# Four low parts of weights on GpSimd, and chunk sums and gated-unit matmuls in fixed turns on TensorE

## The chip, the core and the metric

The kernel runs on one core of one Trainium2 chip. The metric is the device time of one execution in microseconds (us), the median of several. Engines are named as in the profile: PE is TensorE (PEld its weight loads), DVE is VectorE, ACT is ScalarE, POOL is GpSimd, SP is SyncE. Matmuls read their operands from SBUF and write PSUM. Each engine carries out its own queue of instructions in the order in which it was built; an instruction that waits for another engine holds up everything behind it in its queue.

## What is computed

A layer norm of `u` (2048 x 448) feeds two branches whose results are added to `u`:

```python
x  = A_u                       # (1, 2048, 448)
xn = layernorm(x)
# branch A: diagonal state-space convolution, N = 256 states a channel
A  = -exp(log_A_real) + 1j*A_imag;  C = (C_real + 1j*C_imag)*dt
K  = 2*einsum("dn,dnl->dl", C, exp(A*dt*pos)).real      # 448 kernels of length 2048
yA = irfft(rfft(xn, 4096)*rfft(K, 4096))[:2048] + xn*D_skip
# branch B: gated unit, F = 1792
yB = (sigmoid(xn @ w_gate) * (xn @ w_up)) @ w_down
out = x + yA + yB
```

## The kernel before

All matmuls run on values split into a high part, rounded to the `fp32r` format, and a low part, the difference, and add three products (high by high, high by low, low by high).

Two Python generators, `conv()` and `glu()`, put out the work of the branches. The loop at the end of the kernel takes a step of the one that lags behind its share; the number that each `yield` gives says how much work the step held (`WK` = 5.5 for a chunk of `kgen`). A scheduler then makes the order of each engine's queue. It follows the program's order where priorities are equal, but lets an instruction overtake another that it thinks is not ready yet; `hp()` lifts priorities, and `tc.issue_after(ins)` says that an instruction must be queued on its engine behind `ins`. It adds no wait of its own; waits come from the data.

**Branch B** (`glu`, `gate`). The 1792 hidden units come in 14 tiles `f` of 128, in five groups of 3, 3, 3, 3 and 2. The tokens come in two halves of two blocks `t`. In the first half the weights of each tile are loaded into `wraw` (one buffer), ACT makes the high part `wh`, and DVE makes the low part `wl` (L752; L750 for the first tile). In the second half the tiles of `RAW` are loaded again and POOL makes both (L758, L759); the others come back from HBM. `gate` computes one tile for one block: 11 matmuls `gu` for the gate and 11 for the other factor (L698), each group of 11 into one of four PSUM banks shared under the tag `gu`; ACT makes `th`, DVE `hf` (L709), ACT `hh` and DVE `hl` (L716). After a group's tiles, `po` (L811) multiplies by `w_down`, and DVE adds the bank to `acc` (L816).

**Branch A** starts with `prep`, in which DVE and ACT make the parameters of the 448 kernels, and `x_spec`. Then `kgen` makes the kernels in 56 chunks of 8 channels. For chunk `cn`:

- `ahead(cn + 1)`: PE forms phases in `tr` (L526, four matmuls of 512 columns, one PSUM buffer), and ACT takes sines of them into `S` (L535 to L538, two buffers);
- POOL makes magnitudes `me` and `mf` for two chunks at a time (L491, L503), with squares on ACT (L516); once in 8 chunks (`c == 4`) DVE makes `powers` for the next 8 (L440, ten instructions) that those start from;
- DVE multiplies magnitudes and sines: `Et` (L589, L590; two buffers) and `Ft` (L591; one buffer), called the products here;
- PE sums them over the states: `ko`, 32 small matmuls in four column groups (L603), called the chunk's sums;
- after each fourth chunk the bank `ko` is copied, and later `first_stage` puts out 32 matmuls `kp`, `kq` (L553).

A `yield WK / 2` stands between `ahead` and the products, and another after the sums:

```python
                yield WK / 2
                Et = tl[f"Et{cn % 2}"]
                Ft = tl["Ft"]
...
                yield WK / 2
```

Last comes `spectra` (L893, L920, L955), in which the frequency products are formed and transformed back. There the two branches' matmuls already take turns: `sp_mm` holds the last matmul of the branch A, `glu_mm` that of the branch B, each side is queued behind the other with `issue_after`, and the list `glu_on`, filled at the first step of `spectra`, switches this on in `gate` and in the `po` loop.

Of the kernel before, what the change touches and what calls it, by code (L numbers as in the profile page):

```python
# [15 lines left out]
ALU = mybir.AluOpType  # L16
# [13 lines left out]
WK = 5.5  # L30
# [2 lines left out]
WS = 4.5  # L33
WP = 5
WX = 2
HELD = 12.6
HP = 300
Y0 = (8, 1)
# [9 lines left out]
DC = 8  # L48
# [82 lines left out]
def s4d_glu_kernel(ctx, tc, io):  # L131
    nc = tc.nc
    hp = tc.high_priority
    v = nc.vector
# [148 lines left out]
    def x_spec(xn, b0):  # L283

        for p in range(2):
# [7 lines left out]
            for i in range(2):  # L293
                r = row(b0 + i, 2 * p)
                nc.scalar.dma_start(x1_d[:, r : r + 9 : 8], x1[64 * i : 64 * i + 64])
            yield WX

# [147 lines left out]
    def kgen(pk):  # L445
# [72 lines left out]
        def ahead(cn):  # L518
# [19 lines left out]
            sins[:] = [nc.scalar.activation(cs, cs, AF.Sin, scale=-TWO_PI, bias=hpi)]  # L538
            return S

        def first_stage(bank):

            ks, sk = tl["ks"], tl["sk"].rearrange("p k (s r j) -> p r k s j", r=2, j=2)

            pss = [
                psc[-1].tile([128, 8, 2, 32], F32, name="kp", bufs=1),
                psg.tile([128, 8, 2, 32], F32, name="kq", tag="gu", bufs=4),
            ]
            for s_ in range(8):
                for cc in range(2):  # L550
                    for r in range(2):
                        rows = slice(64 * r, 64 * r + 64)
                        nc.tensor.matmul(  # L553
                            pss[r][64 * cc : 64 * cc + 64, s_].rearrange("p j k -> p (j k)"),
                            ks[rows, s_], wk[rows, cc], start=True, stop=True,
                            skip_group_check=True,
                        )
            for r in range(2):
                nc.scalar.copy(sk[:, r], pss[r].rearrange("p s j k -> p k s j"))
            sk_to = sk_d[:, bank // 7, :, bank % 7]  # L560
            nc.scalar.dma_start(sk_to, tl["sk"].rearrange("p (g k) e -> p g (k e)", k=4))
# [11 lines left out]
        for g in range(NCK // NCH):  # L573
            for c in range(NCH):
                cn = g * NCH + c
                S = nxt
                me, mf = (m[:, 2 * DC * (c % 2) : 2 * DC * (c % 2) + 2 * DC] for m in mags)
                if c == 4 and NCH * (g + 1) < NCK:
                    with tc.issue_after(fts[0].ins):
                        powers(pms, g + 1, sins[0])  # L580
                if cn + 1 < NCK:
                    nxt = ahead(cn + 1)
                    if c % 2 == 1:
                        squares(coming[0])
                yield WK / 2
                Et = tl[f"Et{cn % 2}"]
                Ft = tl["Ft"]
                two = lambda ap: ap.unsqueeze(1).to_broadcast([128, 2, 2 * DC, 32])
                v.tensor_tensor(Et[:, :, :, 32:64], two(me[:, :, 32:64]), S[:, 1::-1], ALU.mult)  # L589
                v.tensor_tensor(Et[:, :, :, 0:32], two(me[:, :, 0:32]), S[:, 1:3, :, ::-1], ALU.mult)  # L590
                fts[:] = [v.tensor_tensor(Ft, two(mf), S[:, 3:5], ALU.mult)]  # L591
                if cn + 2 < NCK and c % 2 == 0:
                    coming = magnitudes(cn // 2 + 1)
                if c % 2 == 1:
                    mags = coming
                if cn % 4 == 0:
                    ko = psc[-1].tile([128, 8, 64], F32, name="ko", bufs=1)
                for q in range(2):
                    sl = 2 * (cn % 4) + q
                    for k in range(4):  # L600
                        h, cc = k // 2, k % 2
                        for j in range(4):
                            mm = nc.tensor.matmul(  # L603
                                ko[32 * j : 32 * j + 32, sl],
                                Ft[:, cc, DC * h + 4 * q + j],
                                Et[:, cc, DC * h + 4 * q + j],
                                start=(k == 0),
                                stop=(k == 3),
                                skip_group_check=True,
                            )  # L610
                if cn % 4 == 3:
                    ks = tl["ks"]
                    nc.tensor.matmul(
                        ko[:, :, 0], ident, dm[:, cn // 4], start=False, stop=True, skip_group_check=True
                    )
                    nc.scalar.copy(ks, ko)
                yield WK / 2
                if cn % 4 == 2 and cn > 3 or cn + 1 == NCK:

                    with hp(HP) if cn + 1 == NCK else tc.issue_after(glu_mm[0].ins):  # L620
                        first_stage((cn - 3) // 4 if cn + 1 < NCK else cn // 4)
# [18 lines left out]
    def w_low():  # L640
        return pg.tile([128, 2, 4, 128], F32R, name="wl", bufs=2)
# [77 lines left out]
    def glu():  # L719
        for half in range(2):  # L720
# [4 lines left out]
            for fs_ in ORDER[half]:  # L725
# [14 lines left out]
                for n_, (f, t) in enumerate(order):  # L740
                    if t == 0:
                        wh = pg.tile([128, 2, 4, 128], F32R, name="wh", bufs=2)
                        if half == 0:
                            first = len(raws) == 2
                            raw, rd = raws.pop() if raws else (w_load(f), None)
                            wl = w_low()
                            with hp(HP):
                                nc.scalar.copy(wh, raw)
                                if first:
                                    v.scalar_tensor_tensor(wl, raw, lim[:, 0, 0:1], wh, ALU.mult, ALU.subtract)  # L750
                                else:
                                    v.tensor_tensor(wl, raw, wh, ALU.subtract)  # L752
                            if f not in RAW:
                                for t_, d_ in kept((wh, wl), wt_d, f):
                                    nc.sync.dma_start(d_, t_)
                        elif f in RAW:
                            raw, wl = w_load(f, eng=nc.gpsimd), w_low()
                            nc.gpsimd.tensor_copy(wh, raw)  # L758
                            nc.gpsimd.tensor_tensor(wl, raw, wh, ALU.subtract)  # L759
                        else:  # L760
                            wl = w_low()
                            for t_, d_ in kept((wh, wl), wt_d, f):
                                nc.sync.dma_start(t_, d_)
                        ws.append((wh, wl))
                    between = (lambda s_=mid[n_]: step(*s_)) if cross and mid[n_] else None

                    yield from gate(ws[f - f0], xq[2 * half + t], hs[t], between, half == 0 and (f, t) == (1, 0))
                    if t == 0:
                        dh = pg.tile([128, D], F32R, name="dh", bufs=FCH[0])
                        if half == 0:  # L770
                            rd = rd or rd_load(f)
                            dl = d_low()
                            with hp(HP), tc.issue_after((act if f == 1 else marks)[0].ins):
                                nc.scalar.copy(dh, rd)
                            nc.gpsimd.tensor_tensor(dl, rd, dh, ALU.subtract)
                            if f not in RAW:
                                for t_, d_ in kept((dh, dl), dt_d, f):
                                    nc.sync.dma_start(d_, t_)
                        elif f in RAW:
                            dl = d_low()  # L780
                            rd = rd_load(f, pg.tile([128, D], F32, name="rdw", tag="wraw", bufs=1), nc.gpsimd)
                            nc.gpsimd.tensor_copy(dh, rd)
                            nc.gpsimd.tensor_tensor(dl, rd, dh, ALU.subtract)
                        else:
                            dl = d_low()
                            for t_, d_ in kept((dh, dl), dt_d, f):
                                nc.sync.dma_start(t_, d_)
                        wts.append((dh, dl))
                    yield 1.25
                    for s_ in end[n_] if cross else ():  # L790
                        step(*s_)
                    if cross:
                        yield 2
# [317 lines left out]
    lasts, glu_mm, sp_mm, glu_on, outs, x1s, hfs, xls = [], [], [], [], [0], [0], [], []  # L1111
    xq, psc, raws, acl, marks, slots, pqs = list(x_first), [], [], [], [None, None], {}, []
    W1s, GGs, act = [], [], []
    gens = [conv(), glu()]
    total = [sum(Y0) + 11 * WP + 8 * WX + 34 + NCK * WK + HOLE + 17 * WS, 2 * (4 + NFT * 14.8) - HELD]
    done = [0.0, 0.0]
# [40 lines left out]
```

## Time and profile before

| | us |
|---|---|
| median of 3 runs | 745.98 (745.71 to 748.92) |
| the profiled execution | 749.33 |
| its span, first to last instruction | 747.5 |
| PE busy | 700.4 |
| DVE busy | 561.7 |
| ACT busy | 424.8 |
| POOL busy | 346.7 |

The span falls into these stages: loads, layer norm and `prep` beside the first gate tiles (0 to 126 us), `kgen` beside the gated unit (126 to 560), `spectra` beside the rest of the gated unit (560 to 747.5). Between 275 and 360 us the second half of the tokens is normalised and transposed as well. In the rows of the profile, a line such as L603 is a line of the kernel before, `x56` is a count of instructions, and the part in brackets says how long the engine was idle before the instruction and which engine's instruction ended that wait. A matmul's duration includes its way through the pipeline, so that two that follow each other overlap; the rate is read from a run of many.

### The profile page before, as it was taken

How to read it: one execution, taken by the hardware profiler on the slowest of the kernel's cores; microseconds unless marked ns; L12 is line 12 of the kernel's file. 1: busy time of each engine (PE TensorE's matmuls, PEld its weight loads, DVE VectorE, ACT ScalarE, POOL GpSimd, SP SyncE). 2: the span in 40 equal slices, each digit the busy share in tenths (PEclk: the TensorE clock that was granted, in tenths of full speed). 3: DMA queues.
4: the chain of work that ended last, by engine and by line, in shares of the span. 5: the costliest groups of instructions: out<-in, count | busy, mean ns of one | idle time of the engine just before them, and what ended most of it. 6: DMA issues, size and time to landing. Idle time of an engine off the chain costs nothing.

```text
span 747.5 us, 19396 instructions
## 1 busy us (share of the span) xinstructions
PE 700.4 (94%) x7892; PEld 551.6 (74%) x7892; DVE 561.7 (75%) x776; ACT 424.8 (57%) x651; POOL 346.7 (46%) x423
## 2 busy tenths in 40 slices
PE   3997989998999989899999999999999999999995
PEld 2774868877778778566878887887877777776784
DVE  6899997698879889768778977977864655465533
ACT  3543865677668767697677687767653222323320
POOL 2110036884855966826565586486743200441002
PEclk9998999999999999899999999999999999999998
DMA  9964356253115443365842332232157999999746
GB/s 208 233 186 141 87 171 203 83 179 126 43 52 183 150 118 114 100 182 160 273 140 68 108 93 69 93 96 68 43 159 216 293 249 247 262 253 234 187 107 165
DMA packets 98952, 114.75 MB, mean 154 GB/s; under 512 B 11888, under 2 KB 86832, under 8 KB 98864
## 3 DMA queue, kind: packets, MB, share of 16 engines
q1 hardware_dynamic: 74704, 89.11, 43.5%
q10 hardware_dynamic: 21584, 18.24, 9.0%
q0 software_dynamic: 2576, 6.17, 3.1%
q8 instruction: 62, 1.02, 0.6%
q14 instruction: 26, 0.21, 0.1%
HBM read 69.64 MB, written 43.84 MB: 152 GB/s over the span
## 4 chain that ended last, share of the span: by engine, by line
PE 60%; DMA 13%; DVE 11%; ACT 7%; SPq 4%; issue 4%; ACTq 0%; POOL 0%; DVEq 0%; POOLq 0%
PE gu L698 22%; PE po L811 14%; PE tr L526 6%; PE ko L603 6%; PE sp L893 4%; DMA sx<-x_d 3%; PE pv L920 3%; DMA tb<-in_c_tab_dram 2%; DVE Ft L591 1%; DMA wraw<-in_B_w_gate_dram 1%; ACT S L538 1%; PE kp L553 1%; DMA xe<-in_A_u_dram 1%; DVE Et L589 1%; DVE wl L752 1%
## 5 line engine op out<-in xcount | busy, mean ns | idle before, releaser
L503 POOL TENSOR_TENSOR me<-me,pm 128x32 f32<-128x32 f32 (+1 forms) x168 | 134.0, 797 | 135.2 <-DVE Et L590 122.7
L503 POOL TENSOR_TENSOR mf<-mf,pm 128x64 f32<-128x64 f32 (+1 forms) x112 | 113.9, 1017 | 4.3
L698 PE MATMUL gu<-xh,wh 128*128 128x512 f32 x336 | 98.5, 402 | 5.2 <-DVE hf L709 5.2
L698 PE MATMUL gu<-xh,wl 128*128 128x512 f32 x336 | 100.1, 396 | 0.0
L698 PE MATMUL gu<-xl,wh 128*128 128x512 f32 x336 | 95.9, 391 | 0.0
L589 DVE TENSOR_TENSOR Et<-me,S 128x1024 f32<-128x1024 f32 x56 | 83.3, 1487 | 15.6 <-ACT S L538 15.4
L590 DVE TENSOR_TENSOR Et<-me,S 128x1024 f32<-128x1024 f32 x56 | 74.9, 1338 | 24.4 <-ACT me L516 17.2
L811 PE MATMUL po<-dh,hh 128*128 128x448 f32 x224 | 84.9, 379 | 2.8 <-DVE acc L816 2.1
L811 PE MATMUL po<-dl,hh 128*128 128x448 f32 x224 | 83.0, 371 | 0.0
L811 PE MATMUL po<-dh,hl 128*128 128x448 f32 x224 | 82.8, 371 | 0.0
L535 ACT ACTIVATE S<-tr 128x1024 f32<-128x1024 f32 x56 | 57.5, 1027 | 43.3 <-PE tr L526 41.1
L698 PEld LDWEIGHTS gu<-xh,wh 128*128 128x128 f32 x336 | 62.4, 191 | 23.5 <-DVE hf L709 6.2
L591 DVE TENSOR_TENSOR Ft<-mf,S 128x1024 f32<-128x1024 f32 x56 | 77.7, 1387 | 1.2 <-ACT S L538 0.7
L603 PEld LDWEIGHTS ko<-Et,Ft 128*32 128x32 f32 x3584 | 54.6, 111 | 30.7 <-DVE Ft L591 10.5
L698 PEld LDWEIGHTS gu<-xh,wl 128*128 128x128 f32 x336 | 63.3, 189 | 18.1 <-issue 4.1
L603 PE MATMUL ko<-Et,Ft 128*32 128x64 f32 x3584 | 64.8, 223 | 12.0 <-DVE Ft L591 8.8
L698 PEld LDWEIGHTS gu<-xl,wh 128*128 128x128 f32 x336 | 62.9, 188 | 13.6
L714 ACT CAST hh<-hf 128x512 fp32r<-128x512 f32 x56 | 34.8, 621 | 63.4 <-DVE hf L709 61.1
L526 PE MATMUL tr<-sel,ph 128*128 128x512 f32 x224 | 66.1, 417 | 0.7 <-ACT S L537 0.5
L538 ACT ACTIVATE S<-S,hpi 128x1024 f32<-128x1024 f32 x56 | 65.4, 1168 | 1.2 <-DMA dt_d<-dl 1.2
L816 DVE SCALAR_TENSOR_TENSOR acc<-po,acc 128x448 f32<-128x448 f32 x80 | 47.8, 611 | 22.2 <-PE po L811 22.2
L709 DVE SCALAR_TENSOR_TENSOR hf<-th,gu 128x512 f32<-128x512 f32 x56 | 38.1, 680 | 31.4 <-PE gu L698 27.9
(199 smaller groups left out, 1301.9 us busy)
## 6 DMA issues: line engine op xcount, KB each, us to landing
sk_d<-sk ACTq DMA_DIRECT2D x14, 512.0 KB
sx<-x_d SPq DMA_DIRECT2D x32, 224.0 KB
skl<-sk_d SPq DMA_DIRECT2D x16, 448.0 KB
vp<-v_d SPq DMA_DIRECT2D x16, 448.0 KB
v_d<-vt SPq DMA_DIRECT2D x62, 112.0 KB
wt_d<-wh SPq DMA_DIRECT2D x9, 512.0 KB
wt_d<-wl SPq DMA_DIRECT2D x9, 512.0 KB
wl<-wt_d SPq DMA_DIRECT2D x9, 512.0 KB
```

What stands on the lines that cost most here:

```text
L503: ins = nc.gpsimd.tensor_tensor(m[:, :, w + a : 2 * w : n], m[:, :, a:w:n], par(base + i).unsqueeze(2).to_broadcast([128, 4 * DC, w // n]) ...
L526: nc.tensor.matmul(ps[:, h], ph[:, cn % 2, 128 * h : 128 * h + 128], sel[:, i], start=(i == 0), stop=(i == 1),)
L535: nc.scalar.activation(rows(cs), pv, AF.Abs)
L538: sins[:] = [nc.scalar.activation(cs, cs, AF.Sin, scale=-TWO_PI, bias=hpi)]
L589: v.tensor_tensor(Et[:, :, :, 32:64], two(me[:, :, 32:64]), S[:, 1::-1], ALU.mult)
L590: v.tensor_tensor(Et[:, :, :, 0:32], two(me[:, :, 0:32]), S[:, 1:3, :, ::-1], ALU.mult)
L591: fts[:] = [v.tensor_tensor(Ft, two(mf), S[:, 3:5], ALU.mult)]
L603: mm = nc.tensor.matmul(ko[32 * j : 32 * j + 32, sl], Ft[:, cc, DC * h + 4 * q + j], Et[:, cc, DC * h + 4 * q + j], start=(k == 0), stop=( ...
L698: glu_mm[:] = [nc.tensor.matmul(ps, a_, b_, start=(n == 0), stop=(n == len(mm) - 1))]
L709: marks[1] = v.scalar_tensor_tensor(hf, th, 1.0, pgu[1], ALU.add, ALU.mult)
L811: glu_mm[:] = [nc.tensor.matmul(po, a_[:, bs], w_, start=(n == 0), stop=(n == 3 * fc - 1))]
L816: v.scalar_tensor_tensor(acc[:, b], po, 0.5, acc[:, b], ALU.mult, ALU.add)
```

## The change

Three edits. The low part `wl` of the tiles 2 to 5 is made by POOL in the first half of the tokens, too. In `kgen`, the products and the magnitudes are put out right after `ahead`, without giving the gated unit a step between, and the half step stands between the products and the sums. The sums move into the function `modes`, are queued behind the gated unit's latest matmul, become `sp_mm`, and fill `glu_on`, so that from the first chunk on every matmul of `gate` and `po` is queued behind the latest chunk's sums.

```diff
+EARLY = range(2, 6)
...
+        def modes(ko, Et, Ft, sl):
+            for q in range(2):
+                for k in range(4):
+                    h, cc = k // 2, k % 2
+                    for j in range(4):
+                        mm = nc.tensor.matmul(
+                            ko[32 * j : 32 * j + 32, sl + q],
+                            Ft[:, cc, DC * h + 4 * q + j],
+                            Et[:, cc, DC * h + 4 * q + j],
+                            start=(k == 0), stop=(k == 3), skip_group_check=True,
+                        )
+            return mm
...
                     nxt = ahead(cn + 1)
                     if c % 2 == 1:
                         squares(coming[0])
-                yield WK / 2
+                yield 0
                 Et = tl[f"Et{cn % 2}"]
...
                 if cn % 4 == 0:
                     ko = psc[-1].tile([128, 8, 64], F32, name="ko", bufs=1)
-                for q in range(2):
...
+                yield WK / 2
+                with tc.issue_after(glu_mm[0].ins):
+                    sp_mm[:] = [modes(ko, Et, Ft, 2 * (cn % 4))]
+                glu_on[:] = [1]
                 if cn % 4 == 3:
...
-                                    v.tensor_tensor(wl, raw, wh, ALU.subtract)
+                                    (nc.gpsimd if f in EARLY else v).tensor_tensor(wl, raw, wh, ALU.subtract)
```

In the queues as built, the chunks' work stands as follows. Before, a usual chunk reads on PE: `tr` of the chunk after, 22 matmuls `gu` (or as many `po`), the sums, and the next `tr` at once. After: `tr`, 11 matmuls, the sums, 11 matmuls, the next `tr`. In 12 chunks the sums stood inside the 32 matmuls of `first_stage`; now they stand ahead of them. Between 290 and 375 us of the trace before, where the second half's tokens are transposed, the new queue has `tr` a chunk further ahead of the sums than elsewhere. From `spectra` on, the PE queue is the same. On DVE the products of a chunk stand closer together; on POOL four `wl` are added among the `dl` of the start.

More of the change, by code (lines that the diff above doesn't have):

```diff
@@ L539, in ahead @@
             return S
+        def modes(ko, Et, Ft, sl):
[7 more added lines that the diff above has]
+                            Et[:, cc, DC * h + 4 * q + j],
+                            start=(k == 0),
+                            stop=(k == 3),
+                            skip_group_check=True,
+                        )
+            return mm
         def first_stage(bank):
@@ L597, in kgen @@
                     ko = psc[-1].tile([128, 8, 64], F32, name="ko", bufs=1)
-                for q in range(2):
[L599 to L610, printed above, removed]
+                yield WK / 2
+                with tc.issue_after(glu_mm[0].ins):
+                    sp_mm[:] = [modes(ko, Et, Ft, 2 * (cn % 4))]
+                glu_on[:] = [1]
                 if cn % 4 == 3:
```

## The prediction

> **What bounds the kernel now.** I read the page's parts 1 and 2 first, then the windows view by stage, the waits of PE, and the timeline around single chunks.
>
> ```profile
> PE 700.4 (94%) x7892; PEld 551.6 (74%) x7892; DVE 561.7 (75%) x776; ACT 424.8 (57%) x651; POOL 346.7 (46%) x423
> ...
> PEclk9998999999999999899999999999999999999998
> ```
>
> PE is busy for 94% of the span, so a gain has to come out of PE's idle time and out of the slices in which PEclk, the granted clock, is below 9. The windows view says in which stage these lie (columns: length, then busy time of PE, PEld, DVE, ACT, POOL, granted clock):
>
> ```profile
> 62.00:72.00 10.00, 6.85 (x29) 3.89 (x29) 10.00 (x16) 3.07 (x5) 0.00 (x0) 0.66 0.60 174
> 97.00:115.00 18.00, 12.86 (x61) 9.75 (x59) 17.98 (x23) 11.30 (x23) 10.22 (x6) 1.00 0.70 216
> 126.50:275.00 148.50, 141.15 (x1861) 116.41 (x1860) 123.10 (x129) 105.54 (x150) 108.97 (x125) 0.99 0.39 123
> 275.00:360.00 85.00, 79.22 (x1120) 56.17 (x1119) 70.47 (x83) 65.56 (x107) 51.09 (x65) 0.94 0.50 143
> 360.00:560.00 200.00, 199.07 (x2957) 163.86 (x2950) 158.34 (x164) 140.52 (x199) 123.31 (x147) 1.00 0.35 107
> ```
>
> Three things are to be seen. In the start, DVE sets the pace: it is busy for all of the first two windows while PE waits. In the first half of the chunks PE is idle for 7.35 and 5.78 us. In the second half (360 to 560 us) it is idle for 0.93 us of 200: nothing can be gained there, only lost. PE's waits name what it lacks in the chunks:
>
> ```profile
> PE ko L603 <- DVE Ft L591: 8.8, 6, 2.1
> PE gu L698 <- DVE hf L709: 5.2, 3, 2.0
> PE ko L603 <- DVE Et L589: 3.1, 3, 2.5
> ...
> 279.82 1.51 PE L603 MATMUL ko<-Et,Ft 128*32 128x64 f32 x64 [2.11 <-DVE Ft L591]
> ...
> 191.40:194.80 3.40, 3.40 (x11) 2.89 (x10) 2.90 (x3) 2.08 (x3) 3.24 (x3) 0.53 0.57 157
> 280.10:283.50 3.40, 3.40 (x100) 2.98 (x89) 3.40 (x4) 0.85 (x2) 0.85 (x1) 0.53 0.41 108
> 307.40:314.20 6.80, 6.00 (x74) 3.95 (x75) 5.37 (x5) 2.86 (x6) 4.27 (x6) 0.52 0.46 104
> ```
>
> The chunks' sums wait 8.8 + 3.1 = 11.9 us for their products. Each cluster of such waits is followed by a stretch at about half the clock: 3.4 + 3.4 + 6.8 = 13.6 us, which cost at most half of that, 6.8 us. The second follows a single wait of 2.11 us.
>
> **Four low parts on POOL.** They leave DVE and go to POOL:
>
> ```profile
> 48.87 1.22 DVE L752 TENSOR_TENSOR wl<-wraw,wh 128x1024 fp32r<-128x1024 f32 x1
> ...
> L759 POOL TENSOR_TENSOR wl<-wraw,wh 128x1024 fp32r<-128x1024 f32 x5 | 11.9, 2377 | 0.3
> ...
> 559.12 2.36 POOL L759 TENSOR_TENSOR wl<-wraw,wh 128x1024 fp32r<-128x1024 f32 x1
> ...
> 559.39 2.64 DVE L716 TENSOR_TENSOR hl<-hf,hh 128x512 fp32r<-128x512 f32 x1 [0.68 <-ACT hh L714]
> ...
> 118.82 0.69 DVE L716 TENSOR_TENSOR hl<-hf,hh 128x512 fp32r<-128x512 f32 x1 [0.69 <-ACT hh L714]
> ...
> 34.69 2.21 DVE L248 BATCH_NORM_STATS2 st<-xe 128x6 f32<-128x448 f32 x4 [1.12 <-DMA xe<-in_A_u_dram]
> 36.41 1.14 POOL L775 TENSOR_TENSOR dl<-rd,dh 128x448 fp32r<-128x448 f32 x1 [11.35 <-ACT dh L774]
> ```
>
> DVE gives up 4 x 1.22 = 4.9 us in a stage that it bounds. But the same subtraction takes POOL 2.38 us, and while POOL ran one at 559.12, a subtraction of DVE that takes 0.69 us alone took 2.64 and ended with it: it lost 1.95 us. The statistics at 34.69 went on beside a POOL subtraction. So the price on DVE lies between 0 and 4 x 1.95 = 7.8 us, by what stands in DVE's queue at that moment. The tile 2 falls at about 39 us, where statistics and small instructions stand: I take 0. The tiles 3 and 5 fall among instructions with two inputs from SBUF: 1.95 each. The tile 4 falls among reciprocals with one input: a guess of 0.5. That gives 4.4 of the 4.9 us back: 0.5 us gained, bounds -4.9 to +2.9. Behind each `wl` on POOL stands a `dl`, delayed by up to 2.38 us, which a `po` needs only a group later; SP's next load into `wraw` waits 1.2 us longer, and the tile that it brings is queued tens of matmuls ahead of its use.
>
> **The turns.** The number of matmuls, products and sums is the same, so work itself costs nothing new. What changes is how long PE gives a chunk from its `tr` to its sums. Rates: a run of `gu` and one of `po`; a chunk's sums take 1.10 us, `tr` 1.16, about 1.0 of each before the next can start.
>
> ```profile
> 428.60 4.78 PE gu L698 x21
> ...
> 490.94 3.85 PE po L811 x19
> ```
>
> So `gu` 0.228 and `po` 0.203 us. Before, `tr` to sums held two `tr`, one other chunk's sums and some 44 matmuls: 3 + 44 x 0.228 = 13 us. The new queue holds 33 of them: 10.5 us, from 8.2 to 12 in single chunks. On the other side stands the chain through ACT and DVE. A usual chunk, and three in which DVE makes the `powers`:
>
> ```profile
> 427.43 1.16 PE L526 MATMUL tr<-sel,ph 128*128 128x512 f32 x4
> ...
> 435.38 1.44 DVE L591 TENSOR_TENSOR Ft<-mf,S 128x1024 f32<-128x1024 f32 x1
> ...
> 160.36 1.16 PE tr L526 x4
> ...
> 173.97 1.21 DVE L589 TENSOR_TENSOR Et<-me,S 128x1024 f32<-128x1024 f32 x1
> ...
> 412.57 1.15 PE tr L526 x4
> ...
> 414.58 3.21 DVE L440 SCALAR_TENSOR_TENSOR pm<-pm 128x128 f32<-128x128 f32 x7
> ...
> 417.50 1.14 ACT L538 ACTIVATE S<-S,hpi 128x1024 f32<-128x1024 f32 x1
> ...
> 423.11 1.21 DVE L589 TENSOR_TENSOR Et<-me,S 128x1024 f32<-128x1024 f32 x1
> ...
> 426.31 1.10 PE L603 MATMUL ko<-Et,Ft 128*32 128x64 f32 x64
> ...
> 468.58 1.17 PE tr L526 x4
> ...
> 479.95 1.21 DVE L589 TENSOR_TENSOR Et<-me,S 128x1024 f32<-128x1024 f32 x1
> ```
>
> The usual chunk's products end 436.82 - 427.43 = 9.4 us after its `tr` began; the new queue reaches its sums after 28 `gu` and 3 us, 9.4 us: no wait, and no margin. With `powers`, the chain takes 175.18 - 160.36 = 14.8, 424.32 - 412.57 = 11.8 and 481.16 - 468.58 = 12.6 us. Before, the sums came late enough, as the row at 426.31 shows: 13.7 us after the `tr`, with no wait. In the new queue the three distances are 33 `gu`, 27 `po`, and 16 `gu` with 18 `po`, each with about 3.1 us for the rest: 10.7, 8.6 and 10.4 us. The waits are 4.1, 3.2 and 2.2 us, 3.1 on the mean. Six chunks hold `powers`; in one of them the new queue has `tr` a chunk further ahead, so five wait: 5 x 3.1 = 15.5 us. Products half a step ahead don't shorten this: what delays them in these chunks is the ten `powers` ahead of them and the `acc` among them on DVE, and in the new queue of DVE the `powers` are still ahead. Behind the waiting sums stand eleven `gu` or `po` and the next `tr`, thus ACT and DVE, too: the wait is lost in full, since PE is the bound.
>
> For the 40 or so usual chunks with no margin, small lateness of DVE (a `hf` or `hl` of 0.7 us in between) costs 0 to 0.5 us in some ten of them; I take 4 us in all, bounds 0 and 10. The waits of before, 11.9 us, go: they fell on sums inside `first_stage` or just behind a chunk with `powers`, and these places are gone or have had their wait already. The half-clock stretches of before go as well (-6.8), but five new waits of 2 to 4 us bring one of 3.4 us each, 1.7 us lost: +8.5.
>
> On the clock, the Trainium skill ("TensorE: Matmul & The Clock Gate", Part 1) says that half rate comes back only after a whole idle window of about 3.4 us. The row at 280.10 differs: a wait of 2.11 us was enough. By the page the new waits would mostly cost no clock.
>
> **The sum**: -0.5 + 15.5 + 4 - 11.9 - 6.8 + 8.5 = +8.8 us. From the profiled execution's 749.33 that is 758.1; its time is 3.35 us above the median of 745.98, so in medians 754.8, rounded to 755. The start, `spectra` and its loads keep their queues and shift with PE.
>
> **Rivals.**
>
> *Faster: the waits just go.* If DVE, with the products of a chunk closer together, ends them early enough in the five chunks, the sums come out otherwise: 5w - 6.7 us with w the mean wait there, clock terms as above; it turns at w = 1.3 us. For it: the waits of before all sit where sums were queued badly, and the new order is even. Against it: the row of ten `powers` and the chain of 11.8 us in a stage without contention for PE. With w = 0, 4 us of small waits and no new half clock: -0.5 + 4 - 11.9 - 6.8 = -15.2, 731; with w = 1 and half of the new clock loss, -6.0, 740.
>
> *No change: the clock holds.* The waits come as forecast, but are too short for the clock to fall: without the +8.5 the sum is +0.3, 746. For it: between 97 and 115 us PE was idle for 5.1 us, in waits of up to 2.0 us by the row `gu <- hf`, and the clock stayed at 1.00. Against it: the row at 280.10. It is this that the page named above would have.
>
> *Slower still: POOL holds DVE in the start.* All four `wl` block DVE: +2.9 in place of -0.5, and `hf`, for which `gu` waits 5.2 us there, comes later: 758. It decides if DVE's two-input instructions beside them take over 2 us. The Trainium skill ("GPSIMD Engine Reference", Key points) names the shared SBUF interfaces as a cause of such blocking.
>
> **How the numbers follow.** Forecast 0.48, faster 0.32, no change 0.12, slower still 0.08. Time 755. The range, 732 to 765, takes in the faster case nearly whole, and above it the 6 us more that the usual chunks and the 3.4 us that POOL may cost; the forecast's own range is 750 to 765. This kernel's runs can tell about 0.5%, 3.7 us, from no change; by that, faster has 0.32, the same 0.12, slower 0.56.
>
> **What would show it.** Right: PE's waits on `ko` for `Et` and `Ft` rise from 11.9 to some 20 us, lie at the fifth chunk of each eight, now also between 360 and 560 us, whose PE idle time rises from 0.93 to 5 us or more; more stretches at half clock; on DVE, instructions of over 2 us beside the four `wl`; the end of the parameters at about the same time. Wrong: PE as full as before between 360 and 560 us, and chains of the `powers` chunks of under 10 us.

## The result, and the profile after

The changed kernel takes 765.98 us (median of 6 runs, 762.55 to 772.67) against 746.38 for the kernel before beside it: a ratio of 1.0265, 95% interval 1.0218 to 1.0313. The change makes the kernel slower by 19.6 us, where 9 were forecast. The profiled execution took 767.82 us, its span is 766.0; before it was 749.33 and 747.5.

The page's parts 1 and 2, and the windows view of the changed kernel, first the three stages of the chunks that were shown of before, then four stretches of the clock (columns: length, busy time of PE, PEld, DVE, ACT, POOL, granted clock, DMA share, GB/s):

```profile
PE 704.4 (92%) x7892; PEld 551.2 (72%) x7892; DVE 555.7 (73%) x772; ACT 423.3 (55%) x650; POOL 344.2 (45%) x427
...
PEclk9998999999999999999999999999999999999998
```

```profile
126.50:275.00 148.50, 137.96 (x1780) 113.11 (x1779) 117.96 (x128) 105.23 (x148) 93.06 (x119) 0.98 0.37 118
275.00:360.00 85.00, 77.52 (x1061) 54.55 (x1060) 62.71 (x72) 64.31 (x104) 47.01 (x60) 0.96 0.47 132
360.00:560.00 200.00, 192.42 (x2859) 156.85 (x2859) 158.10 (x169) 135.22 (x192) 114.26 (x148) 1.00 0.35 105
158.60:162.00 3.40, 3.40 (x68) 2.87 (x69) 3.40 (x3) 0.63 (x1) 0.88 (x1) 0.54 0.27 86
237.10:240.50 3.40, 3.17 (x67) 2.81 (x68) 3.40 (x5) 0.74 (x1) 0.18 (x1) 0.54 0.78 225
298.60:302.00 3.40, 3.40 (x9) 2.69 (x10) 2.08 (x2) 1.29 (x2) 0.00 (x0) 0.53 0.32 82
325.90:329.30 3.40, 3.40 (x10) 2.68 (x9) 1.87 (x2) 0.39 (x1) 0.37 (x1) 0.53 0.25 68
```

Between 360 and 560 us, where PE was idle for 0.93 us before, it is idle for 7.58 us now. The waits of PE between 126 and 566 us say what for:

```profile
PE ko L548 <- DVE Et L606: 21.0, 14, 3.8
PE gu L213 <- DVE xl L223: 1.8, 1, 1.8
PE gu L213 <- DVE xr L226: 1.6, 1, 1.6
...
PE ko L548 <- DVE Ft L608: 0.2, 1, 0.2
```

The sums wait 21.2 us for their products, where they waited 11.9. The two `gu` waits, at 324.27 and 350.04 us, belong to the transposes of the second half's tokens, which use the same PSUM tag; before, no wait of PE for `xl` or `xr` stands among those of the chunks. The timeline shows a usual even chunk (number 42 of 0 to 55) on PE, DVE and POOL, with two of the products of the odd chunk ahead of it in the first two DVE rows (the view of PE ends at 474 us, so its last row counts 34 of the 64 sums):

```profile
462.60 1.09 PE L527 MATMUL tr<-sel,ph 128*128 128x512 f32 x4
...
473.52 0.70 PE L548 MATMUL ko<-Et,Ft 128*32 128x64 f32 x34
...
460.85 1.23 DVE L606 TENSOR_TENSOR Et<-me,S 128x1024 f32<-128x1024 f32 x1 [0.23 <-ACT S L539]
...
463.13 1.22 DVE L608 TENSOR_TENSOR Ft<-mf,S 128x1024 f32<-128x1024 f32 x1
...
467.77 2.12 DVE L608 TENSOR_TENSOR Ft<-mf,S 128x1024 f32<-128x1024 f32 x1 [2.75 <-ACT S L539]
469.81 1.65 DVE L607 TENSOR_TENSOR Et<-me,S 128x1024 f32<-128x1024 f32 x1
471.38 2.08 DVE L606 TENSOR_TENSOR Et<-me,S 128x1024 f32<-128x1024 f32 x1
...
463.29 2.40 POOL L504 TENSOR_TENSOR me<-me,pm 128x32 f32<-128x32 f32 x3 [5.04 <-DVE Et L607]
...
468.76 3.62 POOL L504 TENSOR_TENSOR mf<-mf,pm 128x256 f32<-128x256 f32 x2
```

The three products take 1.22 us each in the odd chunk and 2.12, 1.65 and 2.08 in the even one, during which POOL makes the next pair's magnitudes, from 463.29 to 472.38. POOL begins them when the odd chunk's products have let go of the buffer (its row waits for `Et` L607), so they fall beside the next even chunk's work on DVE. The chunk is ready 10.9 us after its `tr`, and the sums start 0.06 us later. In the chunks 33 to 55 the products are ready 10.3 us after `tr` in the even chunks and 8.8 in the odd ones, on the mean. In these chunks the new queue holds 29 `gu` or `po` of the gated unit between `tr` and sums on the mean, where the old one held 40.

### The profile page after: what moved, and what is told of

Same layout as the page of the kernel before. It is cut to its first block, busy times and chain, and to the rows that moved or that the text cites. A ratio compares the mean times of both kernels' runs of the same rounds, so it can differ in the third digit from the quotient of the medians.

```text
span 766.0 us, 19364 instructions
## 1 busy us (share of the span) xinstructions
PE 704.4 (92%) x7892; PEld 551.2 (72%) x7892; DVE 555.7 (73%) x772; ACT 423.3 (55%) x650; POOL 344.2 (45%) x427
## 4 chain that ended last, share of the span: by engine, by line
PE 48%; DVE 24%; ACT 10%; DMA 10%; issue 4%; SPq 1%; ACTq 1%; POOL 0%; DVEq 0%; POOLq 0%
PE gu L706 19%; PE po L819 10%; PE sp L901 5%; PE ko L548 5%; PE tr L527 4%; DVE Et L606 3%; DVE Et L607 3%; DVE Ft L608 3%; DMA v_d<-vt 3%; PE pv L928 3%; DVE hl L724 2%; ACT S L539 2%; DVE pm L441 2%; ACT S L536 2%; DVE acc L824 2%
## 5 line engine op out<-in xcount | busy, mean ns | idle before, releaser
L504 POOL TENSOR_TENSOR me<-me,pm 128x32 f32<-128x32 f32 (+1 forms) x168 | 132.2, 787 | 156.2 <-DVE Et L607 145.3
L706 PE MATMUL gu<-xh,wl 128*128 128x512 f32 x336 | 106.6, 407 | 0.0
L706 PE MATMUL gu<-xh,wh 128*128 128x512 f32 x336 | 101.5, 410 | 2.1 <-DVE hf L717 0.7
L608 DVE TENSOR_TENSOR Ft<-mf,S 128x1024 f32<-128x1024 f32 x56 | 79.4, 1417 | 29.7 <-ACT S L539 25.4
L504 POOL TENSOR_TENSOR mf<-mf,pm 128x64 f32<-128x64 f32 (+1 forms) x112 | 95.3, 851 | 3.0
L606 DVE TENSOR_TENSOR Et<-me,S 128x1024 f32<-128x1024 f32 x56 | 75.3, 1347 | 26.3 <-ACT S L539 26.1
L607 DVE TENSOR_TENSOR Et<-me,S 128x1024 f32<-128x1024 f32 x56 | 73.8, 1318 | 9.2 <-ACT me L517 6.7
L706 PEld LDWEIGHTS gu<-xh,wl 128*128 128x128 f32 x336 | 64.5, 192 | 18.5 <-issue 3.6
L714 ACT ACTIVATE th<-gu 128x512 f32<-128x512 f32 x56 | 33.6, 601 | 57.5 <-PE gu L706 43.1
L527 PE MATMUL tr<-sel,ph 128*128 128x512 f32 x224 | 63.1, 404 | 0.4 <-PE kq L570 0.2
```

The lines of the kernel that those rows point to most:

```text
L504: ins = nc.gpsimd.tensor_tensor(m[:, :, w + a : 2 * w : n], m[:, :, a:w:n], par(base + i).unsqueeze(2).to_broadcast([128, 4 * DC, w // n]) ...
L527: nc.tensor.matmul(ps[:, h], ph[:, cn % 2, 128 * h : 128 * h + 128], sel[:, i], start=(i == 0), stop=(i == 1),)
L706: glu_mm[:] = [nc.tensor.matmul(ps, a_, b_, start=(n == 0), stop=(n == len(mm) - 1))]
```

## The experiments

Each run was compared with the kernel before beside it, which lay between 747.0 and 749.9 us. "Chunk stage" is the time from the first `tr` to the first matmul of `spectra` in the trace: 439.5 us before, 452.1 after. A "stretch" is one of 3.4 us at half clock; before has four in the chunk stage, the changed kernel four.

**One part at a time.** `e1_pool_alone` is the kernel before with the four `wl` on POOL, `e2_no_pool` the changed kernel without that, `e3_products_ahead` the kernel before with the products put out a half step earlier, `e4_turns` the changed kernel without that.

```diff
e1 (on before):  -  v.tensor_tensor(wl, ...)   +  (nc.gpsimd if f in EARLY else v).tensor_tensor(wl, ...)
e2 (on after):   -  EARLY = range(2, 6)        +  EARLY = ()
e3 (on before):  -  yield WK / 2   +  yield 0      (ahead of the products)
                 +  yield WK / 2                   (ahead of the sums)
e4 (on after):   -  yield 0        +  yield WK / 2 (ahead of the products)
                 -  yield WK / 2                   (ahead of the sums)
```

> The kernel before with one part of the change alone: the four wl of tiles 2 to 5 go to POOL; queues as before. After all of the change the first tr came 1.5 us later (128.07 against 126.55 us). If the move of the wl makes that: +1 to +2 us on the time before, and all of it ahead of the first tr. Rival, the move pays by itself (DVE gives up 4.9 us): -2 to -5 us. Rival, it also shifts later stages (another load order, the later spectra stage longer): +4 us or more, with spectra over 175 us from its first matmul to the end (172 before, 177 after).

> The changed kernel with the four wl back on DVE; turns and products ahead stay. If the loss sits in the turns: within 2 us of the changed kernel, +17 to +20 us on the time before, the waits of the sums for Et still 18 to 21 us, the first tr back at 126.5 us. Rival, the wl on POOL cost more than their stage: +12 us or less.

> The kernel before with the products put out half a step ahead and nothing else: sums and gated matmuls in the order in which they were, wl on DVE. If the place of the sums on PE is what costs: within 3 us of the time before, sums' waits for products 8 to 14 us, PE idle under 2 us between 360 and 560 us. Rival, the products ahead of other work on DVE delay hf and hl: +5 to +10 us with PE's waits on hf.

> The changed kernel with the products not ahead: they are queued in the same half step as their sums, the sums still in fixed turns. If the turns make the loss and the products ahead do little: +15 to +25 us on the time before, with PE idle 5 us or more between 360 and 560 us, at even chunks. Rival, the products ahead and the turns only cost together: within 5 us of the time before.

`e3` measured 749.5 us, ratio 1.003 (0.9989 to 1.007), `e4` 764.8 us, 1.0255 (1.0196 to 1.0313). The queues explain it: putting the products out earlier leaves the order on PE, DVE, POOL and SP as it was, in either kernel. So `e3` is the kernel before once more and `e4` the changed one, and the whole loss comes with the turns. The waits of `e4`, and the stage of `spectra` in `e4` and then in the changed kernel:

```profile
PE ko L548 <- DVE Et L606: 21.2, 14, 3.8
...
585.00:690.00 105.00, 104.96 (x801) 79.95 (x802) 57.40 (x115) 29.91 (x57) 28.25 (x35) 1.00 1.05 266
```

```profile
585.00:690.00 105.00, 101.80 (x760) 77.05 (x759) 59.09 (x114) 27.92 (x53) 25.47 (x31) 0.98 1.06 247
```

The waits come out the same to 0.2 us, but from the first matmul of `spectra` to the kernel's last it is 170.2 us here and 176.6 in the profiled execution of the changed kernel (172.1 before, 175.0 in `e3`). What `spectra` adds in the one profile is thus scatter between executions of the same queues, in a stage with a DMA share above 1, and not an effect of the change.

`e1` measured 750.5 us, 1.0045 (1.0016 to 1.0074), with the first `tr` 1.7 us later: the `wl` on POOL cost by themselves, 3.4 us by the ratio and about half of it in the start, where the edit also changes the order of other instructions. The later start holds over all traces: the first `tr` comes at 126.4 to 130.0 us, median 127.2, in the nine with the `wl` on DVE, and at 128.3 to 132.0, median 129.1, in the eight with them on POOL. `e2` missed what was expected: 774.5 us, 1.0373, so with the turns the `wl` on POOL save 8.5 us. The windows of one stage, of `e2` and of the changed kernel, show where:

```profile
345.00:440.00 95.00, 83.42 (x1162) 64.47 (x1166) 67.22 (x84) 59.81 (x92) 42.72 (x63) 1.00 0.47 136
```

```profile
345.00:440.00 95.00, 90.60 (x1293) 71.11 (x1293) 72.01 (x86) 61.54 (x93) 50.97 (x73) 1.00 0.51 146
```

PE is idle there for 11.6 us instead of 4.4, and the chunk stage is 9.4 us longer: its sums wait 27.8 us for their products, and it has six stretches, where the changed kernel has 21.2 us and four. The queue of `e2` has the second half's transposes and the chunks 27 to 36 in another order; that this comes from the planner's other times for the start is argued, not shown.

**The distance from `tr` to the sums.** `e5_sums_late` moves the sums a half step further back, to just ahead of the next `tr`, `e15_sums_early` a quarter step forward; `e6_late_no_pool` is the late form with the `wl` on DVE.

```diff
e5 (on after):   ahead of the sums  -  yield WK / 2  +  yield WK          behind them  -  yield WK / 2  +  yield 0
e15 (on after):  ahead of the sums  -  yield WK / 2  +  yield WK / 4      behind them  -  yield WK / 2  +  yield 3 * WK / 4
e6 (on e5):      -  EARLY = range(2, 6)  +  EARLY = ()
```

> The changed kernel with each chunk's sums a further half step later in the turns (just ahead of the next chunk's tr, instead of in the middle of the step), so that some 13 us lie between tr and sums instead of 10.5. If the distance is too short for the chain through ACT, POOL and DVE: the sums' waits for Et between 360 and 560 us go (PE idle there under 2 us, 7.6 in the changed kernel), and 10 to 15 us of the 19 come back: 750 to 757 us. Rival, turns as such cost (fixed places of sums among gu and po, whatever the distance): still over 762 us.

> As the kernel with the sums a half step later, and with the four wl back on DVE. With the turns as they are, taking the wl from POOL cost 8.5 us more (774.5 us against 766.0); if that was only a worse place of the sums in chunks 27 to 37, it goes with the greater distance: within 3 us of the kernel with the late sums. Rival, wl on POOL help the turns as such: again 6 us or more slower than it.

> The changed kernel with the sums earlier in the step, just behind tr: 17 to 24 matmuls lie between a chunk's tr and its sums, some 8 us, instead of 22 to 33 (10.5 us) or, in the late form, 33 to 45 (13 us). If the distance sets the loss: the chains of 8.1 us (odd) and 10 to 11 us (even) then wait in every even chunk, 2 to 3 us each: 30 us or more above the changed kernel, with waits at half clock on top. Rival, the distance isn't it: within 8 us of the changed kernel.

| | matmuls `gu`, `po` of the gated unit between `tr` and sums in the trace (median of 56 chunks) | chunk stage | median |
|---|---|---|---|
| early (`e15`) | 23 | 476.2 | 790.0 |
| changed kernel | 29 | 452.1 | 766.0 |
| late (`e5`) | 39 | 443.7 | 757.4 |
| late, `wl` on DVE (`e6`) | 39 | 444.9 | 756.5 |
| before | 40 | 439.5 | 746.4 |

The waits and the window of 360 to 560 us, of the late kernel and then of the early one:

```profile
PE ko L548 <- DVE Ft L608: 4.9, 2, 3.3
...
PE ko L548 <- DVE Et L606: 3.0, 2, 2.2
...
360.00:560.00 200.00, 196.08 (x2935) 161.47 (x2934) 165.69 (x172) 141.15 (x199) 121.81 (x149) 1.00 0.35 106
```

```profile
PE ko L548 <- DVE Et L606: 30.0, 17, 4.4
...
PE ko L548 <- DVE Ft L608: 5.7, 9, 1.6
...
360.00:560.00 200.00, 185.31 (x2692) 148.17 (x2691) 145.44 (x159) 126.32 (x182) 105.33 (x141) 0.98 0.34 106
```

The time follows the distance both ways: 6 matmuls less cost 24 us (30 or more were expected), 10 more bring 8.6 back. The expected 10 to 15 us of the late form did not all come (ratio to before 1.0115, 1.0057 to 1.0172): between 360 and 560 us PE is still idle for 3.9 us. `e6` lies at 1.0094 (1.0055 to 1.0132), as `e5` does, so the penalty of `e2` goes with the longer distance.

**POOL's magnitudes.** `e7_no_magnitudes` leaves them out of the changed kernel, `e8_before_no_magnitudes` out of the kernel before, beyond the first two pairs. PE's and DVE's queues stay as they were.

```diff
 def magnitudes(b):
+            if b > 1:
+                return me, mf
```

> The changed kernel with the magnitudes on POOL made for the first two pairs of chunks only and left out for the other 26; all else, PE's and DVE's queues too, as it was. If POOL's instructions hold the products of the even chunks on DVE (they last 4 to 6 us there, 3.5 in the odd ones) and so make the waits: products of 3.5 us in the usual even chunks too, waits of the sums for Et down from 21 to 10 us or less, PE idle between 360 and 560 us 2 to 3 us, left at chunks 36 and 44 with their powers; 8 to 14 us faster than the changed kernel. Rival, the powers on DVE make the waits (as predicted): 0 to 4 us faster, the waits of 1.2 to 3.9 us stay at every fifth chunk of eight.

> The control to the changed kernel without the magnitudes: the kernel before with the magnitudes on POOL made for the first two pairs of chunks only and left out for the other 26, PE's and DVE's queues as they were. If the loss of the change is that its turns let POOL's holding of DVE through to PE, while the queue before has the room for it: 0 to 6 us faster than before, so that the two kernels without magnitudes lie within 5 us of each other. Rival, POOL's magnitudes cost both kernels alike (22 us in the changed one): 15 us or more faster than before.

`e7` measured 743.6 us, 22.4 less than the changed kernel, `e8` 734.9 us, 15 less than before by the ratio of 0.9793 (0.9744 to 0.9841). Waits, window and the group of one product (between 360 and 560 us) of `e7`:

```profile
PE ko L550 <- DVE Et L608: 8.0, 8, 2.1
...
360.00:560.00 200.00, 196.71 (x2995) 160.18 (x2995) 138.44 (x161) 135.83 (x194) 15.37 (x15) 1.00 0.33 101
...
L610 DVE TENSOR_TENSOR Ft<-mf,S 128x1024 f32<-128x1024 f32 x27 | 33.3, 1235 | 21.2 <-ACT S L541 19.5 <-PE ko L550 1.7
```

and waits and window of `e8`:

```profile
PE ko L605 <- DVE Ft L593: 1.7, 3, 1.3
PE ko L605 <- DVE Et L591: 1.6, 2, 1.2
...
360.00:560.00 200.00, 198.70 (x2912) 163.16 (x2913) 139.47 (x165) 133.34 (x192) 19.74 (x24) 1.00 0.33 98
```

POOL's magnitudes are thus behind most of the waits of both kernels: 21.2 us of waits become 8.0 in the one, 11.9 become 3.3 in the other. They act in two ways, and the edit takes away both. POOL holds DVE: without them `Ft` takes 1.24 us instead of 1.36 on the mean between 360 and 560 us, and one of the `powers` 0.29 instead of 0.54. And the products wait for magnitudes that come late: in the changed kernel 0.3, 0.6, 1.6 and 1.1 us, in the chunks 2, 14, 34 and 46. That is at most 3.6 of the 13.2 us that go in the changed kernel, which leaves 9.6 or more to the hold. Fewer waits also mean fewer stretches: one in the chunk stage of `e7`, none in that of `e8`. The control is what keeps this from being too simple. I had expected little from it, and it gained 15 us: what the change adds is not the hold but the lost room for it. In the chunk stage the two kernels lie 12.6 us apart with the magnitudes (452.1 and 439.5) and 6.4 without (430.9 and 424.5): half of the stage's loss needs the magnitudes, and half is there without them, at the distance alone. The 6.4 us are 4.7 of waits and one stretch, 1.7. By the medians somewhat more is left: the two ratios lie 1.5% apart, 11 us, and `e7` has the `wl` on POOL as well. Of the 8.0 us of waits left in `e7`, 3.8 lie at the chunks 12, 20, 36 and 44 with `powers`.

**Moving the hold, moving the powers.** `e12`, `e13` and `e14` make POOL write a column of ones anew ahead of each pair's magnitudes; that has to wait for the even chunk's products, so the magnitudes fall beside the odd chunk's. `e9`, `e10` and `e11` put the ten `powers` out in two halves, in the chunks 3 and 5 of each eight.

```diff
e12 (on before), e13 (on after), e14 (on e6):
                 if cn + 2 < NCK and c % 2 == 0:
+                    if mls:
+                        with tc.issue_after(mls[0].ins):
+                            mls[:] = [nc.gpsimd.memset(me[:, :, 0:1], 1.0)]
                     coming = magnitudes(cn // 2 + 1)
e10 (on before), e9 (on after), e11 (on e6):
-                if c == 4 and NCH * (g + 1) < NCK:
+                if c in (3, 5) and NCH * (g + 1) < NCK:
                     with tc.issue_after(fts[0].ins):
-                        powers(pms, g + 1, sins[0])
+                        powers(pms, g + 1, sins[0], (c // 5,))    # the first five, the last five
```

> The kernel before with one tiny POOL memset (a column of ones, written anew) ahead of each pair's magnitudes, which has to wait until the even chunk's products on DVE are done; so POOL's magnitudes lie beside the odd chunk's products, and the powers of chunk 4 no longer meet them. PE's and DVE's queues are unchanged. If POOL's hold at the even chunks makes the waits of before (at chunks 4, 5, 6, 10, 14, 18, 22): 5 to 12 us faster than before, waits of the sums under 5 us of 11.9. Rival, the hold only moves to the odd chunks or the delayed dl on POOL make po wait: within 3 us of before, or slower.

> The changed kernel with the same memset. If POOL's hold beside the even chunks is the cause there: waits of the sums fall from 21 to 10 us or less, 6 to 14 us faster than the changed kernel (752 to 760 us). Rival: the hold moves to the odd chunks, whose slack of 1 to 3 us doesn't hold it: within 3 us of the changed kernel.

> The kernel with the sums a half step later and the four wl on DVE, with the same memset. If the rest of its loss (7 to 9 us on before) is POOL's hold at chunks 4, 12, 20: 745 to 750 us. Rival, it is tr waiting for ACT and the turns' fixed places: 754 us or more.

> The changed kernel with the ten powers on DVE put out in two halves, ahead of the products of the chunks 3 and 5 of each eight, where the sums have 1 to 4 us of slack, instead of all ten ahead of chunk 4. If powers and magnitudes add up in chunk 4: the waits of some 2 to 4 us at chunks 12, 20, 36, 44 fall below 1.5 us each, and 5 to 10 us come back (756 to 761 us); the even chunks' small waits stay. Rival, POOL alone makes them: within 3 us of the changed kernel.

> The kernel before with the same powers in two halves ahead of chunks 3 and 5. If the waits of before at its chunks with powers come from the ten powers in one place: 3 to 8 us faster than before. Rival, its waits come from the place of the sums beside the first stage: within 3 us of before.

> The kernel with the sums a half step later and the four wl on DVE, with the powers in two halves ahead of chunks 3 and 5. Of the sums' waits of some 8 us left there, about 6 lie at chunks 4, 12 and 20; if the powers and the magnitudes together make them, they go, with a half clock of 3.4 us behind one: 746 to 752 us (756.5 without). Rival, what is left is elsewhere (tr waiting for ACT, another queue): 754 us or more.

| | edit on | median | ratio to before |
|---|---|---|---|
| `e12` hold at odd chunks | before | 752.5 | 1.0057 (1.0016 to 1.0099) |
| `e13` hold at odd chunks | after | 766.0 | 1.0226 (1.0162 to 1.0289) |
| `e14` hold at odd chunks | late, `wl` on DVE | 754.2 | 1.0102 (1.006 to 1.0144) |
| `e9` powers in halves | after | 768.6 | 1.0238 (1.0182 to 1.0294) |
| `e10` powers in halves | before | 755.0 | 1.0092 (1.0051 to 1.0133) |
| `e11` powers in halves | late, `wl` on DVE | 757.3 | 1.0103 (1.0056 to 1.015) |

None of the six gains. In `e13` the waits fall a little, and the time doesn't:

```profile
PE ko L548 <- DVE Et L606: 12.3, 6, 2.6
...
PE ko L548 <- DVE Ft L608: 4.4, 5, 1.8
PE tr L527 <- ACT S L538: 3.2, 2, 2.7
```

The hold did move, as intended: in the chunks 33 to 55 the products take 4.86 us in the odd chunks and 3.88 in the even ones, where they took 3.70 and 4.56. But the odd chunks then run out of their slack (4.6 of the 18.1 us for which the sums still wait), other waits (`tr` for `S`) come in, and the chunk stage has six stretches instead of four, 3.4 us. On the kernel before both edits cost a little (0.6 and 0.9%), on the changed and the late one they stay within the intervals of what they were put on. So shifting the hold or the powers by a chunk gains nothing here; the distance (`e5`, `e15`) and POOL's amount of work (`e7`, `e8`) are what the time followed.

The late form's remaining 7 to 10 us on before is not settled. Its distance is that of before by the median, and neither moving the hold nor the powers took it away. Two things are more frequent in its traces: `tr` waits for `S` 3.8 us in `e5` and 2.1 in `e6`, where it was 0.5 before, and the four late forms have three to six stretches in the chunk stage, where three executions in the old order (before, `e1`, `e3`) have four, two and one. No run separates these. No form that computes everything was faster than the kernel before.

## Why the prediction was wrong

It had the direction, and the mechanism: a shorter way from `tr` to the sums on PE, against a chain that does not get shorter. The size was too small by half. Step by step, the forecast beside the two profiled executions (767.82 - 749.33 = 18.5 us):

| term | forecast | measured |
|---|---|---|
| four `wl` on POOL | -0.5 | +1.5 (the first `tr` comes that much later) |
| waits at chunks with `powers` | +15.5 | +12.0 (1.8, 3.8, 3.2, 1.4 and 1.8) |
| waits at usual chunks | +4 | +9.2, all at even ones |
| old waits | -11.9 | -11.9 |
| old stretches at half clock | -6.8 | -6.8 here; 1.7 and 3.4 were there to save in `e3` and `e1` |
| new stretches | +8.5 | +6.8 (the four rows above, 1.7 each) |
| PE's other waits in the chunk stage | none | +2.4 (4.3 after 1.9; of the 4.3, `gu` for `xl` and `xr` is 3.4) |
| what is left of the chunk stage's 12.6 | none | +0.9 |
| `spectra` and the end | 0 | +4.4 here, scatter by `e4` |

No term makes the miss of 10 us alone. Too small were the usual chunks (5.2), PE's other waits (2.4, put at nothing) and the start (2.0); too large were the chunks with `powers` (3.5). That the sum of the new waits, 19.5 and 21.2 us, came out nearly right is luck: two errors cancel.

**The place of the waits was wrong.** This is the step that failed. The forecast laid 15.5 of 19.5 us of new waits on `powers`, at the fifth chunk of each eight, and 4 on "small lateness" in some ten usual chunks. But 9.2 us lie at usual chunks, and the five chunks with `powers` wait less than forecast. The usual chunk on which the forecast had built its "no margin" (427.43, chunk 38) is an even one with a short chain, 9.4 us; the mean of the even ones before, from chunk 33 on, is 10.7 us, against the 9.4 us of the new distance. What makes the even ones long is POOL's work beside them: without the magnitudes (`e7`) the waits at even chunks other than those with `powers` fall from 9.2 to 4.2 us; 2.1 of these stay at chunk 2, whose magnitudes are still made. The hold lay in the prediction's own rows, which used it for `wl` and `hl`; it was applied to the start and not to the chunks. Chunk 44 shows that it reaches the `powers`, too:

```profile
480.58 1.33 DVE L441 SCALAR_TENSOR_TENSOR pm<-pm 128x128 f32<-128x128 f32 x3
...
482.55 4.33 DVE L441 SCALAR_TENSOR_TENSOR pm<-pm 128x128 f32<-128x128 f32 x6
...
491.16 1.10 PE L548 MATMUL ko<-Et,Ft 128*32 128x64 f32 x64 [1.84 <-DVE Et L606]
```

There POOL makes its magnitudes from 478.73 to 486.42 us, beside the `powers` and not the products: six of them take 0.72 us each, where one takes 0.29 in `e7`. The wait is 1.84 us, 2.2 were forecast.

**The clock of one profile was booked as a gain.** The -6.8 took the four windows of half clock in the one profile of before as the price of its waits, and let them all go with them. But the same wait need not cost one. Row and windows of `e3`, whose queues are those of before, and then windows of before:

```profile
278.71 1.10 PE L604 MATMUL ko<-Et,Ft 128*32 128x64 f32 x64 [2.14 <-DVE Ft L591]
...
274.05:277.45 3.40, 2.52 (x36) 1.91 (x34) 3.15 (x3) 3.31 (x6) 2.31 (x2) 1.00 0.29 80
277.45:280.85 3.40, 2.12 (x103) 1.91 (x104) 3.40 (x5) 1.10 (x2) 0.00 (x0) 1.00 0.29 80
280.85:284.25 3.40, 3.40 (x16) 2.80 (x15) 3.26 (x7) 3.37 (x6) 2.56 (x5) 1.00 0.75 206
```

```profile
276.90:280.30 3.40, 1.29 (x61) 1.02 (x63) 3.40 (x4) 2.39 (x3) 0.65 (x1) 1.00 0.27 74
280.30:283.70 3.40, 3.40 (x87) 2.92 (x76) 3.40 (x5) 1.05 (x2) 1.05 (x1) 0.51 0.41 107
```

This is the wait of 2.11 us of the prediction's row at 279.82, behind which the clock was at half; in `e3` it is 2.14 us and the clock stays at 1.00. In the chunk stage `e3` has one stretch, `e1` two, where the profile of before has four. So of the 6.8 us only 1.7 and 3.4 were there to be saved in these two, and the profile of before, itself 3 us above the median, had more of them. In the comparison of the two profiles this does not show. On the mean of two executions of each order (before and `e3`, the changed kernel and `e4`) the old stretches cost 4.3 us and the new ones 6.8, a net +2.6 where +1.7 was forecast. The sign "more stretches at half clock" did not come in the two profiles, with four in each.

**"The start, `spectra` and its loads keep their queues and shift with PE"** was right for `spectra` and wrong for the start. Two of the four `wl` each held DVE, for longer than was taken:

```profile
40.17 2.32 DVE L262 SCALAR_TENSOR_TENSOR ys<-z,ys 128x8 f32<-128x8 f32 x1
...
43.40 0.17 DVE L262 SCALAR_TENSOR_TENSOR ys<-z,ys 128x8 f32<-128x8 f32 x1
...
49.25 2.51 DVE L312 SCALAR_TENSOR_TENSOR pl<-pl,fr 112x514 f32<-112x514 f32 x4
...
52.27 4.47 DVE L312 SCALAR_TENSOR_TENSOR pl<-pl,fr 112x514 f32<-112x514 f32 x3
...
40.07 2.40 POOL L760 TENSOR_TENSOR wl<-wraw,wh 128x1024 fp32r<-128x1024 f32 x1 [2.51 <-ACT wh L756]
...
49.36 4.67 POOL L760 TENSOR_TENSOR wl<-wraw,wh 128x1024 fp32r<-128x1024 f32 x1 [6.89 <-ACT wh L756]
...
63.50 5.18 POOL L760 TENSOR_TENSOR wl<-wraw,wh 128x1024 fp32r<-128x1024 f32 x1 [7.92 <-ACT wh L756]
...
93.81 6.16 POOL L760 TENSOR_TENSOR wl<-wraw,wh 128x1024 fp32r<-128x1024 f32 x1 [7.19 <-ACT wh L756]
```

The tile 2 was priced at 0, because "statistics and small instructions" stand there: one of these, 0.17 us long elsewhere, became 2.32. Beside the tile 3, priced at 1.95, three `pl` took 4.47 us, where four take 2.51. The measured +1.5 lies inside the bounds of -4.9 to +2.9.

**The rivals.** *The waits just go* did not happen: the mean wait at the five chunks is 2.4 us, above its turning point of 1.3. *The clock holds* is half true: of the five waits of 1.0 to 1.8 us between 360 and 560 us none cost a stretch, the three of 3.2 to 3.8 us earlier did; the fourth stretch stands behind the 1.8 us for `xl`. *POOL holds DVE* named the mechanism behind many of the waits, but in the start, where it costs little.

What the profiles do not explain: of the 19.6 us between the medians, the pairs of executions of the same queues (before and `e3`, the changed kernel and `e4`) carry 16, 14 in the chunk stage and 1.6 in the start. The rest is within the scatter of single executions. Why `gu` waits for `xl` and `xr` in the new order was not tested.

## What to carry to other kernels

Before a fixed turn is given to work that ends a chain over several engines, set the chain's length, for every kind of chunk, against the distance in the new queue: here 6 matmuls less cost 24 us and 10 more returned 9. Where two engines hold each other, look first at who runs beside the chain in each step; emptying POOL gave 15 to 22 us, shifting its work by a chunk gave nothing. And don't book as a gain the clock loss of a single profile: read it in two executions.

## What was unexpected of the hardware

The hold works in both directions, and on small instructions too. The `wl` takes POOL 2.40 us when it starts first, and holds an instruction of DVE of 128x8 elements for 2.15 us; when DVE has two-input instructions back to back, the `wl` itself takes 4.67 to 6.16 us, from 49.36 on by waiting until the four `pl` there are through. The Trainium skill ("SBUF — State Buffer", section "SBUF: two separate sides") has it that the two engines share a pair of ports as a lock: whichever starts first has it for the whole instruction, and the other blocks. The rows agree with that.

The stretches of half clock stand on a grid. From 158.6 us to 237.1, on to 298.6 and on to 325.9 it is 23.0, 18.0 and 8.0 times 3.41 us, and the grid lies otherwise in each execution. The Trainium skill ("TensorE: Matmul & The Clock Gate", Part 1) has a free-running window of 3413 ns, which agrees; that only a whole idle window brings the half rate does not: in before PE is busy for 1.29 of the 3.40 us ahead of the stretch at 280.30. What counts is how much of the wait falls into one window of the grid. The 2.11 us of before lie whole between 276.9 and 280.3; the 2.14 us of `e3` lie across the border at 277.45, with PE idle for 0.88 us of one window and 1.28 of the next. Cut along their grids, the chunk stages of the 17 traces of this case bear that out: 39 windows had PE idle for 1.9 us or more (1.92 the least), and each was followed by a stretch; of 18 with 1.6 to 1.9 us, 7 were; of 77 with 1.0 to 1.6 us, 4, all between 316 and 351 us, where the second half is transposed. Of the 66 stretches in all 16 stand behind windows with less idle time: 11 are the second of two in a row, and 5 lie among the transposes. So the same wait can cost 1.7 us more or nothing, by where the grid lies.
